# Constant matmuls in TensorE's early gaps, first scores in three bank pairs, output weights issued later

## The chip, the cores and the metric

The kernel runs on one core of one Trainium2 chip. The metric is the device time of one execution in microseconds (us). The kernel before takes 421.52 us, the median of eight runs between 418.97 and 425.11.

The engines of the core work in parallel, each through its own list of instructions in a fixed order: TensorE (PE in the profile; PEld is its weight load), VectorE (DVE), ScalarE (ACT), GpSimd (POOL) and SyncE (SP). The last two issue most of the DMA transfers here. TensorE writes its sums to PSUM, which has eight banks; DVE and ACT carry them from there to SBUF.

## The reference

Attention with a squared ReLU in place of the softmax, and then a gated feed-forward layer. There are 8 batches, 12 heads, 448 positions of width 64; the model width is 768 and the hidden width 1536.

```python
scores = scale * np.matmul(q, k.transpose(0, 1, 3, 2))      # scale = 1/sqrt(64)
attn = np.maximum(scores, 0.0) ** 2 / S                      # S = 448
attn_out = np.matmul(attn, v)
x = attn_out.transpose(0, 2, 1, 3).reshape(B * S, H * D)     # 3584 x 768
gate = np.maximum(x @ w_gate, 0.0)
val = x @ w_val
out = gate * val @ w_out                                     # 3584 x 768
```

## The kernel before, in words

**Units of work.** The four heads of a batch that are worked on together are a quad; there are three quads in each of the eight batches. One attention unit is a quad with its 448 query columns. Batch 0 is cut in two parts, the first 192 columns and the other 256, so that work can begin when only a part of q is in SBUF. For a unit the kernel does the following.

- k and q come from DRAM by GpSimd's DMA queue (`load_qk`, line 377, and `dma_in`, line 341), which also turns them to bf16. They are laid out with positions on the partitions and have to be transposed. In batches 0 and 1 TensorE does that (`transpose_first`, line 427, whose matmuls are at line 439; `transpose_pe`, line 455, matmuls at line 464), and DVE or ACT copy the result out of PSUM (lines 413 and 415). From batch 2 on, a DVE copy (the "perm" copy, line 485) and a DMA transpose on SyncE's queue (line 491) do it.
- Scores: seven tiles for a unit, each of four 64x64 matmuls that share the array (line 536). A tile takes a pair of PSUM banks. A ReLU carries it to SBUF (ACT line 546, or DVE line 548), and a square follows there (ACT line 557, or DVE line 559).
- P·V: 28 matmuls over the seven tiles (line 574), and a copy to x (ACT line 589, DVE line 591).

**Feed-forward.** `gv_plain` (matmuls at line 634) makes the gate and value products of batches 0 and 1 in 128-row blocks of the hidden width, with a ReLU on ACT (line 642) and a product on DVE (line 644). Later batches are taken in pairs with seven block products instead of eight (`gv_strassen`, line 734); the output product does the same (`out_both`, line 835). For this, sums and differences of the weights are made once by DVE: those of the gate and value weights into the buffer gvT at line 657 (before that, gvT holds early k, q and v), those of the output weights into the buffer woT at line 674, once all four pieces of the output weights are in SBUF.

**Loads.** All loads from DRAM stand in one list that GpSimd issues in order. It holds batch 0's k and q, its v, the late part of q, then the six pieces of gate and value weights (384 KB each) with batch 1 in between, batch 2's first quad, two pieces of output weights (576 KB each), batch 2's second quad, the other two pieces, batch 2's third quad, and the rest quad by quad. From batch 2 on, there is one buffer for raw k and q, so GpSimd waits for the perm copy before it issues the next quad's, and what stands behind it in the list waits too.

**Order.** The order of every engine is made when the program is built, by a planner (`Planner`, line 56, and `plan`, line 135). It keeps one clock for each engine, assigns a start to each operation from estimated lengths, and at each step commits the operation that can start first. DVE and ACT compete for ReLUs, squares and copies; `BIAS` is added to DVE's end when they are compared. TensorE's choice between attention and feed-forward goes by a share: the feed-forward work that remains before a goal, less `RESERVE` for that segment, is spread over the attention operations before the goal. On the chip only the order remains; the starts come from semaphores.

**PSUM.** Banks are given by the planner. `PAIRS`, `MORE_PAIRS` and `FIRST_PAIRS` are lists of first banks of a pair, for two, three and four pairs:

```python
PAIRS, MORE_PAIRS, FIRST_PAIRS = [0, 2], [0, 2, 4], [0, 2, 4, 6]
```

The whole early work (first transposes, both parts of batch 0's scores and P·V) takes pairs from all four before the change.

Of the kernel before, what the change touches and what calls it, by code (L numbers as in the profile page):

```python
# [55 lines left out]
class Planner:  # L56
    NOUT = 8
    SWITCH = 0.1
    BIAS = 0.3
    MARGIN = 4.0  # L60
    LATE = 3.0
    RESERVE = (1e3, 8.0, 4.0)
    WINDOW, ATT_WINDOW, START, AHEAD = 3, 2, 2.0, 2.0

    def __init__(self):
        self.t = {}
# [65 lines left out]
        self.ops.append(op)  # L132


def plan(first, att, ffn, others, pool, goals):

# [30 lines left out]
    while any(first) or att or ffn or active or pi < len(pool):  # L169
# [47 lines left out]
                cands.append((F[0], F[2], 2, "PE", ffn[F[3]][0]))  # L217
        assert cands, f"no operation can start: {ai} {len(ffn)} {len(active)} {pi}"
        s, _, kind, e, op = min(cands, key=lambda c: c[:3])
        P.commit(op, s, e)  # L220
        done(op)
        if kind == 0:
# [24 lines left out]
def kernel(  # L247
# [74 lines left out]
    def pe(emit, t, **kw):  # L322
        return Op({"PE": (t, t + 0.2)}, emit, **kw)
# [11 lines left out]
    def bank2(among=None):  # L335
        return Buf(r_ps, among if among is not None else PAIRS, width=2)
# [4 lines left out]
    def dma_in(dst, src, n_desc, us, deps=(), alloc=()):  # L341
        op = Op({"POOL": (0.5 + 0.0004 * n_desc,) * 2}, lambda: nc.gpsimd.dma_start(out=dst(), in_=src),  # L342
                deps=deps, alloc=alloc)
        op.load = us
        pool_ops.append(op)
        return op
# [30 lines left out]
    def load_qk(b, g):  # L377
        st = quads[(b, g)] = Quad()
        hs = slice(4 * g, 4 * g + 4)
        early = b < NEARLY  # L380
        st.raw_buf = None if early else Buf(r_raw)
        st.raw = lambda: early_raw(b, g) if early else raw_t[st.raw_buf.idx]
        src = lambda x, t0=0, t1=NT: x[b, hs].rearrange("h (p t) d -> p h t d", t=NT)[:, :, t0:t1]
        k_op = dma_in(lambda: st.raw()[64:128], src(k), 256, 1.15, alloc=[] if early else [st.raw_buf])
        if b == 0:
            st.load_q = lambda t0, t1: dma_in(lambda: st.raw()[0:64, :, t0:t1], src(q, t0, t1), 256, 0.17 * (t1 - t0))
            q_op = st.load_q(0, QT)
        else:
            q_op = dma_in(lambda: st.raw()[0:64], src(q), 256, 1.15)
        st.qk_ops = [k_op, q_op]  # L390
# [36 lines left out]
    def transpose_first(g):  # L427

        st = quads[(0, g)]
        st.qt_buf = Buf(r_qt)  # L430
        ps2, ps2b = bank2(FIRST_PAIRS), bank2(FIRST_PAIRS)

        def emit(ps2, part):
            raw = st.raw()
            for j in range(2):
                for t in range(NT) if part == 0 else range(QT, NT):
                    p0, p1 = (64 if t >= QT else 0, 128) if part == 0 else (0, 64)
                    for h2 in range(2):
                        nc.tensor.transpose(ps_b[64 * h2:64 * h2 + 64, ps2.idx + j, t * 128 + p0:t * 128 + p1],  # L439
                                            raw[p0:p1, 2 * j + h2, t, :], ident[p0:p1, p0:p1])  # L440

        op = pe(lambda: emit(ps2, 0), 0.9, deps=st.qk_ops + [id_op], alloc=[ps2, st.qt_buf])
        kcp = copy_qk(op, ps2, qk_cols(st, 0, NT, 1), qk_banks(ps2, 0, NT, 1), ((0.6, 0.72), (0.83, 0.98)))
        qcp = copy_qk(op, ps2, qk_cols(st, 0, QT, 0), qk_banks(ps2, 0, QT, 0), ((0.30, 0.42), (0.40, 0.55)))
        st.qt_ops = {0: [kcp, qcp]}

        def rest():
            op = pe(lambda: emit(ps2b, 1), 0.45, deps=[st.q_late], alloc=[ps2b])
            cp = copy_qk(op, ps2b, qk_cols(st, QT, NT, 0), qk_banks(ps2b, QT, NT, 0), ((0.37, 0.5), (0.51, 0.66)))
            st.qt_ops[HALF] = [kcp, cp]  # L450
            return op

        return op, rest
# [471 lines left out]
    def make_ident():  # L925
# [5 lines left out]
        for i in range(4):  # L931
            for c0, c1 in ((0, 32 * i), (32 * i + 32, 128)):
                if c0 < c1:
                    nc.vector.memset(ident[32 * i:32 * i + 32, c0:c1], 0.0)

    id_op = Op({"DVE": (1.5, 1.6)}, make_ident)
    others.append(id_op)
    for g in range(NQ):
        load_qk(0, g)
    for g in range(NQ):  # L940
# [8 lines left out]
            load_v(1, "abc".index(x))  # L949
    load_qk(2, 0)  # L950
    load_v(2, 0)
    for par in range(2):
        for hf in range(2):
            load_out(par, hf)
        load_qk(2, 1 + par)
        load_v(2, 1 + par)
    for b in range(3, B):
        for g in range(NQ):
            load_qk(b, g)
            load_v(b, g)  # L960


    att = []
    done_at = {}
    A_ = [Attention(0, g, 0, HALF, FIRST_PAIRS) for g in range(NQ)]
    A_ += [Attention(0, g, HALF, S - HALF, FIRST_PAIRS) for g in range(NQ)]
    A_ += [Attention(b, g, pairs=MORE_PAIRS if b < 4 else PAIRS) for b in range(1, B) for g in range(NQ)]

# [20 lines left out]
    for n in range(NQ, len(A_)):  # L989
        if n < 2 * NQ:  # L990
            att.append(late[n - NQ]())
        for i in range(NT):
            att.append(A_[n].s(i))
            if i == 1 and n not in (NQ, 2 * NQ):
                PV(n - 1)
            if i == 1 and n >= 2 * NQ - 1:
                T(n + 1 - NQ)
        if n in (2 * NQ - 1, len(A_) - 1):
            PV(n)
        if n == 2 * NQ - 1:  # L1000
            part_two = len(att)
# [10 lines left out]
        out_both(2 * p, p + 2, To_ops)  # L1012
        goals.append(done_at.get(2 * p + 3))

    for op in plan(first, att, ffn, others, pool_ops, goals):
        op.emit()


# [28 lines left out]
```

## Time and profile before

| | |
|---|---|
| median of eight runs | 421.52 us (418.97 to 425.11) |
| profiled execution | 419.79 us, of which the span from first to last instruction is 418.0 us |
| TensorE busy | 396.0 us, 95% of the span |
| DVE, ACT busy | 324.0 us (77%), 264.6 us (63%) |
| mean granted TensorE clock | 0.994 |
| DMA | 43.44 MB, 104 GB/s over the span |

The page of a profile cuts the span into 40 equal slices and shows for each, in tenths, how busy an engine was. The lists of instructions in order of time have the start, the length, the engine, the line, the operation with what it writes and reads, and in brackets the idle time before it with what ended that. Matmuls of one row may overlap, and the end of a matmul is modelled: the time from one start to the next tells more than one length.

### The profile page before, as it was taken

How to read it: one execution, taken by the hardware profiler on the slowest of the kernel's cores; microseconds unless marked ns; L12 is line 12 of the kernel's file. 1: busy time of each engine (PE TensorE's matmuls, PEld its weight loads, DVE VectorE, ACT ScalarE, POOL GpSimd, SP SyncE). 2: the span in 40 equal slices, each digit the busy share in tenths (PEclk: the TensorE clock that was granted, in tenths of full speed). 3: DMA queues.
4: the chain of work that ended last, by engine and by line, in shares of the span. 5: the costliest groups of instructions: out<-in, count | busy, mean ns of one | idle time of the engine just before them, and what ended most of it. 6: DMA issues, size and time to landing. Idle time of an engine off the chain costs nothing.

```text
span 418.0 us, 8710 instructions
## 1 busy us (share of the span) xinstructions
PE 396.0 (95%) x3444; PEld 208.9 (50%) x3444; DVE 324.0 (77%) x585; ACT 264.6 (63%) x408; POOL 73.9 (18%) x119
## 2 busy tenths in 40 slices
PE   3797999989999999999999999999999999999995
PEld 2475665434455544444445554444445555555562
DVE  1758777997699988999888779888878847677552
ACT  2778876987586876877864568776665443433221
POOL 7736303222111222211111022201000000000000
PEclk9999899999999999999999999999999999999999
DMA  8999989975579999789869778654002340000144
GB/s 117 184 199 200 200 136 166 154 101 78 83 100 180 154 184 126 79 92 103 112 88 107 162 143 147 87 68 64 1 2 59 94 115 0 2 0 2 39 114 114
DMA packets 75737, 43.44 MB, mean 104 GB/s; under 512 B 37808, under 2 KB 75696, under 8 KB 75696
## 3 DMA queue, kind: packets, MB, share of 16 engines
q0 software_dynamic: 33328, 23.60, 42.1%
q1 hardware_dynamic: 42368, 19.28, 27.6%
q8 instruction: 27, 0.44, 0.4%
q14 instruction: 14, 0.11, 0.1%
HBM read 47.19 MB, written 11.01 MB: 139 GB/s over the span
## 4 chain that ended last, share of the span: by engine, by line
PE 88%; DMA 4%; ACT 4%; DVE 2%; issue 1%; POOL 0%; DVEq 0%; ACTq 0%; POOLq 0%
PE ps L734 35%; PE ps L835 24%; PE ps L634 12%; PE ps L536 9%; PE ps L574 7%; DMA qkT<-perm 2%; ACT at L546 1%; DMA gvT<-in_q_dram 1%; ACT qkT L413 1%; PE ps L439 1%; PE ps L464 1%; DVE at L548 1%; DVE qkT L415 1%; ACT at L557 1%; POOL gvT L342 0%
## 5 line engine op out<-in xcount | busy, mean ns | idle before, releaser
L546 ACT ACTIVATE at<-ps 128x896 bf16<-128x896 f32 (+2 forms) x125 | 100.6, 845 | 21.5 <-PE ps L536 21.2
L683 ACT COPY f<-ps 128x448 f32<-128x448 f32 x101 | 53.3, 533 | 46.7 <-PE ps L734 43.9
L559 DVE TENSOR_TENSOR at<-at 128x896 bf16<-128x896 bf16 (+2 forms) x123 | 66.3, 562 | 6.4 <-ACT at L546 5.7
L548 DVE TENSOR_SCALAR at<-ps 128x896 bf16<-128x896 f32 (+2 forms) x64 | 61.7, 969 | 5.7 <-PE ps L536 5.5
L557 ACT ACTIVATE at<-at 128x896 bf16<-128x896 bf16 (+2 forms) x66 | 58.3, 892 | 5.0 <-DVE at L548 4.3
L536 PE MATMUL ps<-qkT 64*64 64x448 bf16 (+2 forms) x756 | 55.0, 353 | 5.5 <-ACT qkT L413 1.7
L734 PE MATMUL ps<-xT,gvT 128*128 128x448 bf16 x216 | 52.8, 353 | 0.5 <-ACT f L683 0.5
L734 PE MATMUL ps<-sx,wv 128*128 128x448 bf16 x216 | 52.8, 353 | 0.0
L734 PE MATMUL ps<-xT,wg 128*128 128x448 bf16 x216 | 52.5, 353 | 0.0
L734 PEld LDWEIGHTS <-gvT 128*128 128x128 bf16 x324 | 30.4, 98 | 31.8 <-issue 5.3
L835 PE MATMUL ps<-wo,hT 128*128 128x384 bf16 x240 | 44.1, 326 | 0.0
L835 PEld LDWEIGHTS <-hT 128*128 128x128 bf16 x312 | 29.9, 98 | 22.5 <-issue 3.1
L685 ACT ACTIVATE f<-ps 128x384 f32<-128x384 f32 x37 | 18.2, 493 | 36.1 <-PE ps L835 33.4
L342 POOL DMA_DIRECT2D vv<-in_v_dram x44 | 26.3, 608 | 74.8 <-PE ps L536 65.4
L835 PEld LDWEIGHTS <-sh 128*128 128x128 bf16 x288 | 27.2, 98 | 21.5 <-issue 3.8
L536 PEld LDWEIGHTS <-qkT 64*64 64x64 bf16 x756 | 19.6, 108 | 34.6 <-issue 27.9
L574 PE MATMUL ps<-at,vv 64*64 64x448 bf16 (+2 forms) x700 | 35.8, 345 | 0.3 <-ACT at L557 0.3
L634 PE MATMUL ps<-xT,wg 128*128 128x448 bf16 (+2 forms) x180 | 32.5, 316 | 2.2 <-ACT xT L589 1.5
L342 POOL DMA_DIRECT2D raw<-in_k_dram x18 | 11.3, 626 | 120.7 <-DVE perm L485 120.1
L634 PE MATMUL ps<-xT,wv 128*128 128x448 bf16 (+2 forms) x180 | 32.2, 315 | 0.0
L825 DVE SCALAR_TENSOR_TENSOR o<-ps,f 128x384 f32<-128x384 f32 x40 | 22.2, 554 | 11.8 <-PE ps L835 8.9
L734 PEld LDWEIGHTS <-wg 128*128 128x128 bf16 x216 | 20.4, 98 | 20.9 <-issue 3.2
(60 smaller groups left out, 479.9 us busy)
## 6 DMA issues: line engine op xcount, KB each, us to landing
out_dram<-o SPq DMA_DIRECT2D x112, 96.0 KB, 2.2
vv<-in_v_dram POOLq DMA_DIRECT2D x44, 112.0 KB, 5.8
raw<-in_k_dram POOLq DMA_DIRECT2D x18, 224.0 KB, 4.8
raw<-in_q_dram POOLq DMA_DIRECT2D x18, 224.0 KB, 6.7
wg<-in_moe_w_gate_dram POOLq DMA_DIRECT2D x6, 384.0 KB, 9.7
wv<-in_moe_w_val_dram POOLq DMA_DIRECT2D x6, 384.0 KB, 10.8
wo<-in_moe_w_out_dram POOLq DMA_DIRECT2D x4, 576.0 KB, 10.9
gvT<-in_k_dram POOLq DMA_DIRECT2D x6, 224.0 KB, 8.1
```

The costliest lines, as they stand in the source:

```text
L342: op = Op({"POOL": (0.5 + 0.0004 * n_desc,) * 2}, lambda: nc.gpsimd.dma_start(out=dst(), in_=src), deps=deps, alloc=alloc)
L536: nc.tensor.matmul(ps[64 * j:64 * j + 64, ps2.idx + h2, :n], lhsT=self.k_of(j, h2, i), rhs=self.q_of(j, h2), start=True, stop=True)
L546: nc.scalar.activation(self.at_of(i), src, AF.Relu)
L548: nc.vector.tensor_scalar_max(self.at_of(i), src, 0.0)
L557: nc.scalar.activation(at, at, AF.Square)
L559: nc.vector.tensor_tensor(at, at, at, ALU.mult)
L574: nc.tensor.matmul(ps[64 * h2:64 * h2 + 64, ps2.idx + j, :n], lhsT=st.v_of(j, h2, c), rhs=self.at_of(c)[64 * j:64 * j + 64, h2, :], start= ...
L634: nc.tensor.matmul(ps[:, pb.idx, :n], lhsT=w[:, kd, fc], rhs=xT_t[xbuf[b].idx][:, kd, cols], start=(kd == 0), stop=(kd == KD - 1))
L683: nc.scalar.copy(dst, src)
L734: nc.tensor.matmul(ps[:, pb.idx, :S], lhsT=w(g)[:, fc], rhs=rhs, start=start and g == 0, stop=stop and g == KH - 1, skip_group_check=True)
L825: op = Op({"DVE": V384}, lambda: nc.vector.scalar_tensor_tensor(o_t[ob.idx], ps[:, pb.idx, :OH], float(out_scale), f_t[fb.idx][:, :OH], AL ...
L835: nc.tensor.matmul(ps[:, pb.idx, :OH], lhsT=lhs(kf), rhs=rhs(kf), start=start and kf == 0, stop=kf == FH - 1, skip_group_check=True)
```

## The change

There are four parts.

1. **Fillers.** The planner gets a function `filler`. When the operation that it has chosen for TensorE could start only after a gap, and its planned start is below `FILL_UNTIL` (21 us on the planner's clock), it first commits a number of full-array matmuls (128x128 weights, up to 448 columns) that write to bank 6 or 7 and that nobody reads. Their operand is a stretch of ones in woT, set by one new DVE memset; woT's own contents are written much later. The columns are counted at 1200 a us while the planner's clock is below `FILL_COLD` (4 us), and at 2400 after. In the built program there are 48 such matmuls: 11 of 443 columns ahead of everything, 5 of 393 after the first quad's transposes, three groups of 3 (373, 439 and 428 columns) up to the second score tile of the second quad, then one or two between most score tiles (250 to 400), 7 of 418 ahead of the third P·V, and one of 243 ahead of the first gate matmul.
2. **Bank pairs.** The first transposes and the first part's scores and P·V take three pairs, so banks 6 and 7 stay free for the fillers. The second part keeps four.
3. **Loads.** The pieces of the output weights are spread: one, batch 2's second quad, two, batch 2's third quad, one.
4. **Planner's numbers.** `BIAS` 0.3 to 0.2; `RESERVE` 8 and 4 to 4 and 3; the estimated transfer of the second quad's k 1.15 to 2.4. `PV_AT` and `T_AT` name a 1 that stood in the code.

The planner makes a new order of all engines from this. In the early part it moves the second quad's transposes behind five of the first quad's seven score tiles, and the third quad's behind all seven; before, the second quad's came ahead of all score tiles and the third quad's after three.

```diff
-    BIAS = 0.3
+    BIAS = 0.2
-    RESERVE = (1e3, 8.0, 4.0)
+    RESERVE = (1e3, 4.0, 3.0)
+    FILL_FROM, FILL_COLD, FILL_UNTIL, FILL_MARGIN = 0.4, 4.0, 21.0, 0.1
...
         s, _, kind, e, op = min(cands, key=lambda c: c[:3])
+        if e == "PE" and s < P.FILL_UNTIL:
+            t0 = max(P.t.get("PE", 0.0), P.FILL_FROM)
+            gap = s - t0 - P.FILL_MARGIN
+            f = filler(gap, t0 < P.FILL_COLD) if gap > 0.1 else None
+            b = f.alloc[0].pick(t0) if f is not None else None
+            if b is not None and b[0] <= t0:
+                P.commit(f, t0, "PE")
+                P.mode = op.mode
         P.commit(op, s, e)
...
-        k_op = dma_in(lambda: st.raw()[64:128], src(k), 256, 1.15, alloc=[] if early else [st.raw_buf])
+        k_op = dma_in(lambda: st.raw()[64:128], src(k), 256, 2.4 if (b, g) == (0, 1) else 1.15,
+                      alloc=[] if early else [st.raw_buf])
...
-        ps2, ps2b = bank2(FIRST_PAIRS), bank2(FIRST_PAIRS)
+        ps2, ps2b = bank2(MORE_PAIRS), bank2(FIRST_PAIRS)
...
+    still = woT.rearrange("p a f m -> p (a f m)")
+    still_op = Op({"DVE": (0.2, 0.3)}, lambda: nc.vector.memset(still[:, :S], 1.0))
+    def filler(us, cold):
+        pb = bank([6, 7])
+        total = int(us * (1200 if cold else 2400))
+        n = (total + S - 1) // S
+        width = max(64, total // n)
+        def emit():
+            for _ in range(n):
+                nc.tensor.matmul(ps[:, pb.idx, :width], lhsT=still[:, :128], rhs=still[:, :width], start=True, stop=True)
+        return pe(emit, us, deps=[still_op], alloc=[pb], reads=[pb])
...
-    for par in range(2):
-        for hf in range(2):
-            load_out(par, hf)
-        load_qk(2, 1 + par)
-        load_v(2, 1 + par)
+    load_out(0, 0)
+    load_qk(2, 1)
+    load_v(2, 1)
+    load_out(0, 1)
+    load_out(1, 0)
+    load_qk(2, 2)
+    load_v(2, 2)
+    load_out(1, 1)
...
-    A_ = [Attention(0, g, 0, HALF, FIRST_PAIRS) for g in range(NQ)]
+    A_ = [Attention(0, g, 0, HALF, MORE_PAIRS) for g in range(NQ)]
```

## The prediction

> **What bounds the kernel now.** I read the page's slices first, then stretches, TensorE in order of time, GpSimd's queue, and the chain of work that ended last.
>
> ```profile
> PE   3797999989999999999999999999999999999995
> DVE  1758777997699988999888779888878847677552
> ACT  2778876987586876877864568776665443433221
> PEclk9999899999999999999999999999999999999999
> ```
>
> TensorE has room in the first five slices (52 us) and in the last one; in between it is the bound. The stretches give the size (the column after the lengths is TensorE's busy time):
>
> ```profile
> 0.00:10.45 10.45, 3.47 (x66) 2.58 (x68) 1.90 (x11) 2.22 (x3) 8.08 (x17) 1.00 0.87 117
> 10.45:20.90 10.45, 7.54 (x131) 4.46 (x127) 7.89 (x24) 8.14 (x19) 8.18 (x12) 1.00 1.35 184
> 20.90:31.35 10.45, 9.47 (x188) 8.00 (x183) 5.62 (x15) 7.84 (x18) 4.12 (x6) 1.00 1.39 199
> 31.35:41.80 10.45, 8.02 (x190) 6.21 (x184) 8.82 (x19) 9.16 (x19) 6.39 (x9) 0.97 1.39 200
> 41.80:52.25 10.45, 9.54 (x130) 7.21 (x128) 8.35 (x14) 8.71 (x14) 4.13 (x6) 0.87 1.35 200
> ```
>
> 38.0 of 52.25 us are busy, so 14.2 us stand idle there; from 60 us to the last output matmul the list of TensorE's waits holds only 3.0 us. What a change saves before 50 us arrives at the end nearly whole; later there is little to save. The fourth-last and last columns matter too: the clock column says 1.00 until 41 us, and DMA moves 180 to 200 GB/s from 10 us on. TensorE in order of time contradicts the clock column:
>
> ```profile
> 5.66 1.70 PE L439 MATMUL ps<-ident,gvT 128*64 128x128 bf16 x28 [5.66 <-DMA gvT<-in_q_dram]
> ...
> 19.97 2.45 PE L574 MATMUL ps<-at,vv 64*64 64x192 bf16 x56
> ...
> 24.33 0.72 PE L634 MATMUL ps<-xT,wg 128*128 128x192 bf16 x6
> 24.90 0.66 PE L634 MATMUL ps<-xT,wv 128*128 128x192 bf16 x6
> ...
> 37.80 0.97 PE L464 MATMUL ps<-ident,gvT 128*64 128x128 bf16 x28
> ...
> 41.75 1.71 PE L464 MATMUL ps<-ident,gvT 128*64 128x128 bf16 x28
> ```
>
> 28 transposes take 0.97 us at 37.80 and 1.71 us at 41.75, where the granted clock reads 0.50 to 0.54. The first transposes take 1.70, although the column says 1.00 there: they run at half speed. So does the first P·V: 14 rounds of four 192-column matmuls in 2.3 us are 0.163 us a round, 192 columns at 1.2 a ns; at 24.90 six 192-column matmuls start 0.082 us apart, 2.4 a ns. Half speed therefore lasts from 5.66 to about 24 us, and again from 41.0 to 44.5.
>
> GpSimd's queue tells when weights land, since in the built program each issue waits for the transfer eight before it:
>
> ```profile
> 19.37 0.60 POOL L342 DMA_DIRECT2D gvT<-in_v_dram  x1 [1.34 <-DMA wg<-in_moe_w_gate_dram]
> 21.37 0.59 POOL L342 DMA_DIRECT2D gvT<-in_v_dram  x1 [1.40 <-DMA wv<-in_moe_w_val_dram]
> ...
> 38.16 0.59 POOL L342 DMA_DIRECT2D vv<-in_v_dram  x1 [0.76 <-PE ps L536]
> 39.30 0.59 POOL L342 DMA_DIRECT2D vv<-in_v_dram  x1 [0.55 <-PE ps L536]
> ...
> 64.26 1.72 POOL L342 DMA_DIRECT2D wo<-in_moe_w_out_dram  x2
> ```
>
> The first gate and value pieces land at 19.37 and 21.37, one 384 KB piece every 2.0 us. By the same order of eight, k and q of batch 1's second quad land by 38.16 and 39.30 (the scores named there were long done). These times are DMA's own; the change leaves their order.
>
> ```profile
> 75.21 10.39 DMA qkT<-perm
> 85.60 0.04 issue
> 85.64 0.57 PE ps L536 x8
> ```
>
> In the chain, one DMA transpose of 10.39 us is the only large wait after 60 us; TensorE stands 1.28 us for it.
>
> **The change, step by step.**
>
> *Fillers.* 48 matmuls of 128x128 constants. First 11 of 443 columns, from about 1.1 us (DVE starts at 0.83; its new memset of 448 columns is near the 0.17 us row of the 128x128 one). At half speed 11 x 443 / 1.2 = 4.06 us, ending at 5.2, before the data at 5.63: free. The other 37 have 12,898 columns: 5.4 us at full speed, 10.7 us at half. They stand ahead of scores, P·V and transposes in TensorE's fixed order, so what overruns its gap delays these.
>
> Is the clock full by then? The Trainium skill (TensorE: Matmul & The Clock Gate, Part 1) has a free-running 3.4 us activity window and says not to care: the ramp costs under 1% of a typical span. By that rule one window at half speed is the whole loss, at most 1.7 us. The rows say otherwise: scores in small bursts kept it half for 18 us. The lost time is 3 x 0.65 us in transposes and about 1.8 us in P·V (21 rounds of 0.163 instead of 0.080). I go by the rows. The window does bear on the filler: 4.06 us covers a whole window only for some phases, so I take full speed from about 7 us, and half speed until 14 as the bad end. Part 4 of the same page says that transposes do not engage the full clock; 0.97 against 1.71 us contradicts it here.
>
> *First scores in three bank pairs and the new order.* Before, the second quad's transposes came ahead of all scores, and the third quad's (12.23) waited for a bank pair. Now five of the first quad's seven score tiles come ahead of the second quad's transposes, two more ahead of the third's. Walk: transposes at 5.66, about 1.5 us; the two copies still follow each other, now DVE 896 (0.62, row at 54.91) then ACT 384 (0.48) instead of 0.91 + 0.36; scores at 8.4 instead of 9.98, first relu at 8.6 instead of 11.22. Five tiles pass while the second quad's data (landed 8.65) waits; its transposes run at about 9.6, copies to 11.6; the third's need the pair these copies free: 11.7 to 12.6. The eighth tile starts at 12.6; before it was at 16.1. From there ACT has about ten relus at 0.39 (4.32/11), three squares at 0.52 and a copy: 6.0 us, to 18.7; DVE's 4 relus of 0.53, 15 squares of 0.28 and copy come to the same. The last two tiles' P·V (0.6) and x copy (0.5) end near 20.9, instead of 24.7. With three pairs rather than four, two relus still run side by side, which is all that the engines can do; I cost it at nothing, and at up to 1 us if a late relu stops the order. At half speed until 14 us the fillers take 1.64, 0.93 and 1.10 us in these gaps and the eighth tile comes at 15.4: 0.6 us gained in all.
>
> *What is late next.* The first value matmul (24.90) can move to 21.4 where its weights land: 3.5 us. The next weights (25.37 against a use at 29.07, 29.37 against 33.76) allow as much. Batch 1's second quad, used at 41.75 and landed at 39.30, allows 2.45: TensorE then stands about 1 us there. So 2.45 us is carried on. The half-speed spell at 41 to 44.5 lies past the fillers' end. It costs 0.7 (transposes) + 0.3 (scores) + 0.35 (P·V) = 1.4 us, and whether it returns depends on how idle gaps fall in the window: 0 to 1.4, I take 0.7, as two ends equally near.
>
> *Output weights.* The four 576 KB pieces were issued two at 48 and two at 64 us; now it is one, two, and the last behind batch 2's third quad at about 75. It adds 576 KB at 197 GB/s, 2.9 us, to the DMA time beside the 10.39 us transpose. If both share, the wait of 1.28 us grows by up to 2.9; if the transpose is ahead, by nothing, and a lighter queue at 48 can shorten it to a gain of 0.5. I take 0.6 lost, nearer to the small end: only its tail overlaps.
>
> *BIAS, RESERVE, the k estimate.* They add no instruction but re-deal work: 67 relus from PSUM on DVE instead of 64; 2.6 and 4.6 us more FFN matmuls ahead of two P·Vs of batch 1. There TensorE idled only 0.2 us (50 to 60), so nothing to win; 3.0 us of waits after 60 could vanish or double. From -1.5 to +3; I take 0.
>
> *Sum.* 419.79 (span 418.0 and 1.8 around it) - 2.45 - 0.7 + 0.6 = **417.2**. The eight runs fall into 418.97 to 420.26 (with the profiled one) and 422.78 to 425.11; the median, 421.52, lies between the groups and no view shows what parts them. I forecast 417.2 for the median too, as the cold start is the part that could differ run by run; if the groups recur it is 418.9.
>
> **Rivals.** (1) *More*: the spell at 41 us vanishes whole and the landing at 39.30 is no hindrance because copies and relus catch up meanwhile: 3.5 + 1.4 gives 414.9. For it: the idle 0.92 us at 45.5 waits for an ACT copy. Against: TensorE's order is fixed there. (2) *Swallowed*: weights and data land as before, the clock stays half until 14, or stage two stays bound by ACT and DVE (8.82 and 9.16 of 10.45 us): 0 to 0.6 us gained, 419.2 to 421.5. (3) *Slower*: DVE reaches the differences of the output weights (line 674) before the last piece has landed and, being in order and full (75 to 95 us: 19.8 of 20), holds back every hidden-tile product. The piece is issued near 75 and lands in 9.4 to 12.6 us, by 87.6; DVE gets there about 4.8 us after the third perm copy (86.63 less 2.6), at 88.8. From a landing 13.8 us after issue it costs; beyond 16.4 it eats the gain; 22.3 us would make it 425.7. Against it: no such transfer took over 12.6.
>
> **Numbers.** Forecast 0.60 (own range 415 to 419.5, about half of it under 417.3), more 0.22, swallowed 0.12, slower 0.06. About 1% (4.2 us) is what these runs can tell from no change. Faster 0.28 + 0.22 = 0.50, same 0.44, slower 0.06. Range 413.8 to 421.5: down to rival 1 with 1 us of re-dealing, up to rival 2's end.
>
> **What would show it.** Right: transposes near 1 us from the second quad on; first relu near 8.6; eighth tile near 12.6; first value matmul near 21.4, waiting for DMA; transposes of batch 1's second quad near 39.4, waiting for DMA; TensorE full from 47 us about 3 us sooner. Wrong: fillers or the P·V at 0.16 us a round after 14 us; a wait over 3 us at the second DMA transpose of batch 2; DVE idle ahead of line 674.

## The result, and the profile after

The changed kernel takes 417.97 us, the median of 22 executions, where the kernel before takes 422.21 (59 executions in the same comparison). The ratio is 0.992, with a 95% interval from 0.9894 to 0.9946. So the change saves 0.8%, some 3.3 us of the kernel before: the interval excludes no change, but the gain is under the 1% that the prediction took as the least that these runs can tell. Ratios and intervals here use only the executions within 1.5% of the fastest of their kernel, the medians all of them, so that a ratio is not the quotient of two medians. One execution of each kernel lay far off (584.96 us at a mean granted clock of 0.655, and 517.8).

The others scatter by 6 to 7 us, with TensorE's mean granted clock. In a second comparison, 21 of 55 executions of the kernel before have a clock of 0.996 or more and a median of 419.3 us, and the others 423.5; of 20 of the changed kernel, nine have such a clock and 417.1 us, and the others 419.1. Among the executions at 0.996 or more the change is thus worth 2.2 us.

The profile below is of an execution of the changed kernel that took 419.0 us, with a span of 417.2. In the spans the gain over the profiled execution before (418.0) is only 0.8 us; one execution in the middle of the scatter says little by its length, but its rows say where time went. First the page's slices, TensorE, DVE, ACT and clock:

```profile
PE   8997999989999998999999999999999999999995
DVE  4759686989799988989788879898986847677552
ACT  3678677876677777876675668776756644433221
PEclk9999999999999999999999999999999999999999
```

TensorE now looks busy from the first slice on, but part of that is constants. In stretches (length; TensorE's busy time first, then weight loads, DVE, ACT, GpSimd, granted clock, DMA share, GB/s):

```profile
0.00:10.45 10.45, 8.62 (x95) 4.27 (x99) 4.30 (x18) 3.50 (x6) 7.87 (x17) 1.00 0.88 115
10.45:20.90 10.45, 9.52 (x180) 5.18 (x179) 7.55 (x20) 7.21 (x18) 8.34 (x12) 1.00 1.36 187
20.90:31.35 10.45, 9.41 (x191) 7.62 (x189) 6.30 (x15) 7.90 (x19) 3.52 (x5) 1.00 1.39 199
31.35:41.80 10.45, 8.12 (x172) 6.57 (x175) 9.46 (x20) 9.06 (x17) 6.02 (x9) 0.92 1.39 199
41.80:52.25 10.45, 10.39 (x118) 7.41 (x120) 6.60 (x12) 6.47 (x12) 4.26 (x7) 0.92 1.35 200
```

46.06 us are busy of 52.25, where it was 38.03; but 12.2 of the 46.06 are the constants. TensorE in order of time (start, length, instruction, idle time ahead):

```profile
1.39 4.25 PE L962 MATMUL ps<-woT 128*128 128x443 bf16 x11 [1.39 <-DVE woT L949]
5.79 1.18 PE L451 MATMUL ps<-ident,gvT 128*64 128x128 bf16 x28
...
9.52 1.07 PE L451 MATMUL ps<-ident,gvT 128*64 128x128 bf16 x24
...
11.88 1.03 PE L451 MATMUL ps<-ident,gvT 128*64 128x128 bf16 x22 [0.40 <-DVE qkT L427]
...
17.36 0.28 PE L548 MATMUL ps<-qkT 64*64 64x192 bf16 x4
17.57 0.39 PE L962 MATMUL ps<-woT 128*128 128x250 bf16 x2
...
19.05 1.32 PE L586 MATMUL ps<-at,vv 64*64 64x192 bf16 x56
...
20.39 1.41 PE L962 MATMUL ps<-woT 128*128 128x418 bf16 x7
21.73 0.77 PE L586 MATMUL ps<-at,vv 64*64 64x192 bf16 x28
...
23.29 0.66 PE L646 MATMUL ps<-xT,wv 128*128 128x192 bf16 x6
...
40.09 1.70 PE L476 MATMUL ps<-ident,gvT 128*64 128x128 bf16 x28 [0.88 <-DVE at L571]
41.73 1.71 PE L586 MATMUL ps<-at,vv 64*64 64x256 bf16 x28
...
43.64 0.89 PE L646 MATMUL ps<-xT,wg 128*128 128x256 bf16 x6
```

The first 28 transposes take 1.18 us (1.70 before), 22 of the third quad's 1.03 (1.53 before): from the second quad on the clock is full. P·V runs 14 rounds in 1.32 us (2.45 before). The first value matmul is at 23.29, 1.6 us sooner, and TensorE goes over to the feed-forward blocks of 256 columns at 43.64, where it did at 46.41, with 24 score tiles done behind the first value matmul where it had done 26. Two tiles are some 0.5 us (12 matmuls, three tiles, take 0.7), so it is 2.3 us ahead. At 40.09 the transposes take 1.70 us again; the second half-speed spell has not gone. Later, waits come back:

```profile
73.25 0.57 PE L548 MATMUL ps<-qkT 64*64 64x448 bf16 x8 [1.27 <-DMA qkT<-perm]
...
86.52 0.57 PE L548 MATMUL ps<-qkT 64*64 64x448 bf16 x8 [0.74 <-DMA qkT<-perm]
```

Before, TensorE waited for a DMA transpose once in the whole span; now three times, 3.2 us in all. Between 56 and 100 us it stands 2.33 us, where it stood 1.29. DVE, in the same kernel, makes the copies that feed these transposes:

```profile
60.41 0.62 DVE L497 COPY perm<-raw 128x1792 bf16<-128x1792 bf16 x1
...
73.33 0.63 DVE L497 COPY perm<-raw 128x1792 bf16<-128x1792 bf16 x1 [1.48 <-DMA qkT<-perm]
...
86.60 0.63 DVE L497 COPY perm<-raw 128x1792 bf16<-128x1792 bf16 x1 [1.40 <-DMA qkT<-perm]
```

The second and third copies wait until the transposes of the copy before them have read the buffer. The third starts at 86.60; before the change at 86.63. TensorE had been 2.3 us ahead at 44 us; this chain had gained nothing by its third copy.

### The profile page after: what moved, and what is told of

Same layout as the page of the kernel before. It is cut to its first block, busy times and chain, and to the rows that moved or that the text cites. A ratio compares the mean times of both kernels' runs of the same rounds, so it can differ in the third digit from the quotient of the medians.

```text
span 583.2 us, 8812 instructions
## 1 busy us (share of the span) xinstructions
PE 573.6 (98%) x3492; PEld 249.9 (43%) x3492; DVE 338.0 (58%) x586; ACT 269.6 (46%) x408; POOL 73.9 (13%) x119
## 4 chain that ended last, share of the span: by engine, by line
PE 97%; DVE 1%; ACT 1%; DMA 1%; issue 0%; POOL 0%; POOLq 0%
PE ps L746 37%; PE ps L847 25%; PE ps L646 14%; PE ps L548 9%; PE ps L586 9%; PE ps L962 1%; PE ps L451 1%; DMA gvT<-in_q_dram 1%; PE ps L476 0%; DVE at L560 0%; ACT qkT L425 0%; ACT at L558 0%; DVE qkT L427 0%; POOL gvT L353 0%; DVE xT L603 0%
## 5 line engine op out<-in xcount | busy, mean ns | idle before, releaser
L746 PE MATMUL ps<-sx,wv 128*128 128x448 bf16 x216 | 74.4, 468 | 0.0
L746 PE MATMUL ps<-xT,gvT 128*128 128x448 bf16 x216 | 74.4, 469 | 0.0
L746 PE MATMUL ps<-xT,wg 128*128 128x448 bf16 x216 | 74.2, 469 | 0.0
L548 PE MATMUL ps<-qkT 64*64 64x448 bf16 (+2 forms) x756 | 64.1, 407 | 1.4 <-DVE qkT L427 1.1
L847 PE MATMUL ps<-wo,hT 128*128 128x384 bf16 x240 | 63.6, 429 | 0.0
L586 PE MATMUL ps<-at,vv 64*64 64x448 bf16 (+2 forms) x700 | 48.1, 433 | 0.2 <-DVE at L560 0.2
L646 PE MATMUL ps<-xT,wv 128*128 128x448 bf16 (+2 forms) x180 | 46.4, 412 | 0.0
L646 PE MATMUL ps<-xT,wg 128*128 128x448 bf16 (+2 forms) x180 | 44.4, 402 | 0.9 <-ACT at L558 0.6
L746 PEld LDWEIGHTS <-wv 128*128 128x128 bf16 x216 | 24.5, 118 | 36.5 <-issue 34.5
L803 DVE CUSTOM_DVE_ANT_0 g<-ps,f 128x448 bf16<-128x448 f32 x36 | 22.5, 624 | 30.2 <-PE ps L746 27.6
```

The source lines that it names most:

```text
L548: nc.tensor.matmul(ps[64 * j:64 * j + 64, ps2.idx + h2, :n], lhsT=self.k_of(j, h2, i), rhs=self.q_of(j, h2), start=True, stop=True)
L586: nc.tensor.matmul(ps[64 * h2:64 * h2 + 64, ps2.idx + j, :n], lhsT=st.v_of(j, h2, c), rhs=self.at_of(c)[64 * j:64 * j + 64, h2, :], start= ...
L646: nc.tensor.matmul(ps[:, pb.idx, :n], lhsT=w[:, kd, fc], rhs=xT_t[xbuf[b].idx][:, kd, cols], start=(kd == 0), stop=(kd == KD - 1))
L746: nc.tensor.matmul(ps[:, pb.idx, :S], lhsT=w(g)[:, fc], rhs=rhs, start=start and g == 0, stop=stop and g == KH - 1, skip_group_check=True)
L803: cur["g1"] = Op({"DVE": V448}, lambda pb=cur["D"], f=u2, gb=cur["g1b"]: nc.vector._custom_dve(dve_ops.TENSOR_ADD_SAT, out=g_t[gb.idx], in ...
L847: nc.tensor.matmul(ps[:, pb.idx, :OH], lhsT=lhs(kf), rhs=rhs(kf), start=start and kf == 0, stop=kf == FH - 1, skip_group_check=True)
```

## The experiments

Each ratio is against executions of the kernel before on the same chip, taken together with those of the variants. Three chips were used, and the kernel before took 421.87 us on the first (the changed kernel again, no_fill, start_alone, wo_early), 423.06 on the second (drop_small, late_fill, no_retune, perm2) and 423.6 on the third (retune_alone, bias_only, wo_early_2, late_wo). The table has the rows that the text uses, from each kernel's profile: start of the first value matmul, start of the transposes of batch 1's second quad with the length of 28 of them, DVE's third permuting copy, TensorE's waits for DMA transposes.

| kernel | first value | batch 1, second quad | third copy | waits | span | median (n) | ratio, 95% |
|---|---|---|---|---|---|---|---|
| before | 24.90 | 41.75 (1.71) | 86.63 | 1.3 | 418.0 | | 1 |
| changed, again | 23.29 | 40.09 (1.70) | 86.60 | 3.2 | 417.2 | 417.9 (20) | 0.9951, 0.992 to 0.9981 |
| no_fill | 25.77 | 42.54 (0.97) | 91.31 | 5.0 | 420.5 | 423.23 (20) | 1.0026, 0.9992 to 1.006 |
| start_alone | 24.93 | 41.48 (0.97) | 87.58 | 5.2 | 421.7 | 422.96 (20) | 1.0023, 0.9991 to 1.0054 |
| wo_early | 23.97 | 40.11 (0.97) | 86.57 | 2.4 | 415.8 | 416.33 (4) | 0.9882, 0.9803 to 0.996 |
| wo_early_2 | 22.95 | 39.49 (1.70) | 86.10 | 1.4 | 415.6 | 417.7 (12) | 0.9922, 0.988 to 0.9965 |
| drop_small | 23.56 | 39.70 (0.97) | 87.94 | 5.5 | 419.5 | 420.69 (10) | 0.9987, 0.9941 to 1.0033 |
| late_fill | 23.18 | 40.20 (0.97) | 86.08 | 2.9 | 415.3 | 418.81 (10) | 0.992, 0.989 to 0.9949 |
| no_retune | 25.67 | 42.22 (0.97) | 85.83 | 2.5 | 418.9 | 423.13 (10) | 1.0032, 0.9992 to 1.0072 |
| retune_alone | 22.70 | 39.05 (0.97) | 84.31 | 1.0 | 414.1 | 417.56 (12) | 0.9921, 0.988 to 0.9961 |
| bias_only | 23.13 | 39.27 (0.97) | 88.20 | 4.6 | 418.4 | 420.84 (12) | 0.999, 0.9947 to 1.0034 |
| late_wo | 23.17 | 40.20 (0.97) | 84.41 | 1.5 | 414.9 | 416.49 (10) | 0.9896, 0.9854 to 0.9938 |

**The changed kernel again.** Not edited; it gives the profile shown above.

> The changed kernel as it is, for a profile at the full clock. Theory of the prediction: transposes near 1 us from the second quad on, first relu near 8.6 us, eighth score tile near 12.6, first value matmul near 21.4 waiting for its weights, transposes of batch 1's second quad near 39.4 waiting for DMA, TensorE full from 47 us; 417 to 418 us. Rival (the gain is lost on the way, or comes from elsewhere): first value matmul as early, but the transposes of batch 1's second quad within 1 us of 41.75.

It took 417.9 us. Its ratio is 0.9951, and its interval (0.992 to 0.9981) overlaps that of the first comparison (0.9894 to 0.9946).

**No constants.** The order is that of the changed kernel, but the fillers emit nothing.

```diff
-            for _ in range(n):
+            for _ in range(0):
```

> The changed kernel with the fillers' matmuls left out and every other instruction in the same order. Theory clock (the fillers' full clock is what saves): the first P.V at 0.16 us a round again, transposes 1.6 us, and most of the gain gone, within 1 us of the kernel before. Theory order (the new order of scores and transposes saves, the clock little): half speed until about 24 us, but first relu near 8.6 and the eighth tile near 14, and a gain of 2 us or more kept.

```profile
9.90 1.54 PE L451 MATMUL ps<-ident,gvT 128*64 128x128 bf16 x22
...
19.72 2.45 PE L586 MATMUL ps<-at,vv 64*64 64x192 bf16 x56
...
25.77 1.17 PE L646 MATMUL ps<-xT,wv 128*128 128x192 bf16 x6
```

TensorE in order of time: at half speed from the first transposes to the first value matmuls (six of 192 columns take 1.17 us, then 0.66), and the whole gain is gone. In this order of work the constants are needed, and their effect is the clock.

**The first filler alone.** The kernel before with only the 11 matmuls of 443 columns ahead of the transposes.

```diff
+    def warm_emit():
+        for _ in range(11):
+            nc.tensor.matmul(ps[:, 7, :443], lhsT=still[:, :128], rhs=still[:, :443], start=True, stop=True)
+    warm = Op({"PE": (0.1, 0.2)}, warm_emit, deps=[still_op])
...
+    trans = [warm, *trans]
```

> The kernel before with only the first eleven 443-column constant matmuls put ahead of its transposes. Theory clock: the first transposes or those of the second quad run in 1 us, but the clock falls back in the gaps that follow; P.V at 0.16 again; 0 to 1 us gained. Rival (one busy window is enough[...]): full speed from about 7 us to the end, P.V at 0.08 us a round, 2 us gained. If neither: no speed gained and no time.

```profile
1.39 4.25 PE L943 MATMUL ps<-woT 128*128 128x443 bf16 x11 [1.39 <-DVE woT L937]
5.57 1.69 PE L439 MATMUL ps<-ident,gvT 128*64 128x128 bf16 x28
...
19.88 2.45 PE L574 MATMUL ps<-at,vv 64*64 64x192 bf16 x56
```

In this execution 4.25 us of constants, right up to the transposes, leave them at half speed (1.69 us), and P·V as well. In the changed kernel the same filler was followed by 1.18. No time is gained: 422.96 us. The profiled execution, at a mean clock of 0.998, is not like most: of the 19 others 18 have 0.970 to 0.983, where the kernel before has 0.984 to 1.0. So the filler did change the granted clock, but how fast the first transposes and P·V ran in those 18 no profile shows. A burst at the start without the fillers behind it is worth nothing here.

**Small gaps unfilled.** Fillers of gaps under 0.3 us emit nothing.

```diff
-            for _ in range(n):
+            for _ in range(n if us > 0.3 else 0):
```

> The changed kernel without the fillers of gaps under 0.3 us (the 250- to 400-column ones between score tiles and the last one of 243), everything else in order. In the changed kernel's profile eleven score tiles from 14.2 us on come 0.53 us apart with TensorE busy throughout; without fillers it was 0.36. Theory (TensorE's fillers and its changes between 64x64 and full-array matmuls pace these tiles): 0.35 to 0.40 us a tile, first P.V near 17.2 to 17.8 instead of 19.05, first value matmul near 21.7. The end moves by less than 0.5 us, since the second quad of batch 1 still waits for its data near 40. Rival (they hold the clock): the clock falls to half before P.V, P.V at 0.16 us a round, first value matmul no earlier than 23.3, the end 1 us later or more.

```profile
14.42 1.60 PE L548 MATMUL ps<-qkT 64*64 64x192 bf16 x20 [0.41 <-ACT qkT L425]
16.21 2.14 PE L548 MATMUL ps<-qkT 64*64 64x192 bf16 x24 [0.19 <-DVE at L560]
18.29 2.40 PE L586 MATMUL ps<-at,vv 64*64 64x192 bf16 x56
...
42.45 0.97 PE L646 MATMUL ps<-xT,wg 128*128 128x256 bf16 x6
```

I had expected the tiles to come closer, and they did: 0.35 us apart, eleven in 3.87 us, where the fillers made it 4.82 (0.53 from one to the next where a filler stands between). But the clock fell in that stretch, P·V took 2.40 us, and the value matmul came at 23.56, no sooner than with the fillers (23.29). So far the rival was right: the small fillers cost about 0.2 us where one stands between two tiles, 1 us in all, and hold the clock for it. That this is why the kernel ends later (420.69 us) is not shown. In its profile TensorE goes over to the blocks of 256 columns at 42.45, 1.2 us ahead of the changed kernel, whose profile has the half-speed spell at 40 us; behind that it stands 5.5 us for DMA transposes, where the changed kernel stands 3.2. And its interval (0.9941 to 1.0033) overlaps that of the changed kernel again.

**The second half-speed spell.** Three constant matmuls of 448 columns ahead of batch 1's first score tile, three ahead of the transposes of its second quad.

```diff
+            if (b, g) == (1, 1):
+                fill_bank(ps2.idx, 3)
...
+                if (self.b, self.g, i) == (1, 0, 0):
+                    fill_bank(ps2.idx, 3)
```

> The changed kernel with six more constant matmuls of 448 columns: three ahead of batch 1's first score tile, three ahead of the transposes of its second quad, where TensorE stood 0.9 us. Theory (the half-speed spell near 41 us comes from these gaps, and parts the runs of the changed kernel into 416 to 418.5 and 420.5 to 422): no spell, fewer runs over 420, median 0.5 to 1.5 us lower. Rival (the spell is not in the gaps, or comes back a window later): the same spread; the six matmuls cost up to 0.5 us.

28 transposes take 0.97 us at 40.20 and there is no spell. The median is 418.81 us, the ratio 0.992, as for the changed kernel, with a narrower range: 417.09 to 420.25, against 416.16 to 422.01. But the profiles of seven kernels that have nothing against it show the transposes at full speed as well, and wo_early lacks the spell where wo_early_2, the same kernel, has it. It comes and goes from one execution to the next. The six matmuls cost 1.5 us of TensorE, about what the spell was estimated at.

**The loads back in their old order.**

```diff
-    load_out(0, 0)
-    load_qk(2, 1)
...
-    load_out(1, 1)
+    for par in range(2):
+        for hf in range(2):
+            load_out(par, hf)
+        load_qk(2, 1 + par)
+        load_v(2, 1 + par)
```

> The changed kernel with the output weights' four pieces loaded where the kernel before loads them. Theory of the prediction (the late piece costs 0.6 us at the second DMA transpose of batch 2): 0.5 us faster than the changed kernel, the wait for that transpose about 1.3 us shorter or gone. Rival (spreading the pieces takes pressure off the perm copies and helps): 0.5 to 2 us slower than the changed kernel, with a longer wait for batch 2's k and q.

The first timing, 416.33 us, had four executions; the repeat had twelve.

> The changed kernel with the order of loads of before, again, as its first timing rested on four executions. If the later output weights cost the 0.6 us that the prediction took: about 417.3, 0.6 under the changed kernel. If they cost nothing: 417.5 to 418.5. If they are worth something: over 418.5. The waits for the DMA transposes of batches 2 and 3 (1.4 and 0.6 us) stay as in its first profile.

417.7 us in the repeat, against 417.9 and 417.97 for the changed kernel in other comparisons: no difference that these runs can show. The wait for the transposes does not go with the late piece either: with the old order it is 2.4 and 1.4 us, with the new 3.2.

**Two permuting buffers.** N_PERM 2 instead of 1, and four output buffers instead of five to make room.

```diff
-    N_QT, N_AT, N_X, N_F, N_G, N_O = 3, 10, 3, 5, 4, 5
-    N_RAW, N_PERM, N_VV = 1, 1, 3
+    N_QT, N_AT, N_X, N_F, N_G, N_O = 3, 10, 3, 5, 4, 4
+    N_RAW, N_PERM, N_VV = 1, 2, 3
```

> The changed kernel with two buffers for the perm copy instead of one (and four output buffers instead of five, for the room). TensorE's order stays as it is up to the fourteenth P.V. In the changed kernel's profile the waits for DMA transposes are 3.2 us against 1.3 before, and the perm copy waits for the transpose ahead of it. Theory (one perm buffer ties each transpose to the end of the last, and this chain takes back part of the gain): these waits under 1 us, 1.5 to 2.5 us faster than the changed kernel. Rival (the transposes are slow because the loads share the DMA engines, so that two at once only slow each other): waits of 3 us as before, no gain.

422.51 us in ten executions, five from 416.43 to 422.13 and five from 422.89 to 426.67. The ratio, 0.9895 (0.984 to 0.995), rests on the first five alone; the profile, with one wait of 5.1 us for a transpose, is of the slowest. The scatter is wider than the gain looked for, and the one change of buffers came with another: inconclusive.

**The planner's numbers back.** The changed kernel with BIAS 0.3 and RESERVE 8 and 4.

```diff
-    BIAS = 0.2
+    BIAS = 0.3
...
-    RESERVE = (1e3, 4.0, 3.0)
+    RESERVE = (1e3, 8.0, 4.0)
```

> The changed kernel with BIAS at 0.3 and RESERVE at 8 and 4 again. Theory of the prediction (they re-deal work and are worth nothing): within 1 us of the changed kernel. Rival (they give part of the gain, by the feed-forward moved ahead in batch 1 or the ReLUs dealt to DVE): 1 to 3 us slower than the changed kernel.

This was not expected: 423.13 us, nothing left of the gain, though fillers, bank pairs and loads are all there and the clock is full (P·V 1.35 us). The first value matmul is at 25.67, later than before the change. (bias_only below has the same kernel but for BIAS.)

**The planner's numbers alone.** The kernel before, with those two lines of the change and nothing else.

```diff
-    BIAS = 0.3
+    BIAS = 0.2
...
-    RESERVE = (1e3, 8.0, 4.0)
+    RESERVE = (1e3, 4.0, 3.0)
```

> The kernel before with BIAS 0.2 and RESERVE 4 and 3 only: no fillers, no third bank pair, the old order of loads. Theory one (these constants re-deal relus between DVE and ACT, which pays only where the early part is no longer held at half speed): first value matmul still near 24.9 us, time within 1% of before, 419 to 423. Theory two (the constants are the gain by themselves, as the loss on taking them back could say): 416 to 419, and TensorE's idle time after 50 us smaller. The prediction's own value was 0 with bounds from 1.5 us faster to 3 us slower.

The whole gain: 417.56 us, a ratio of 0.9921 (0.988 to 0.9961), with not one constant matmul. Its TensorE in order of time, after two rows of the kernel before that have not been shown yet:

```profile
12.23 1.53 PE L439 MATMUL ps<-ident,gvT 128*64 128x128 bf16 x22 [1.38 <-DVE at L548]
...
15.78 4.18 PE L536 MATMUL ps<-qkT 64*64 64x192 bf16 x56 [1.38 <-DVE at L548]
```

```profile
7.97 1.53 PE L439 MATMUL ps<-ident,gvT 128*64 128x128 bf16 x22 [0.76 <-DMA gvT<-in_q_dram]
...
10.89 1.53 PE L439 MATMUL ps<-ident,gvT 128*64 128x128 bf16 x22 [0.75 <-ACT qkT L413]
...
13.82 4.44 PE L536 MATMUL ps<-qkT 64*64 64x192 bf16 x56 [0.75 <-ACT qkT L413]
18.35 2.27 PE L574 MATMUL ps<-at,vv 64*64 64x192 bf16 x56
...
22.70 0.66 PE L634 MATMUL ps<-xT,wv 128*128 128x192 bf16 x6
...
39.05 0.97 PE L464 MATMUL ps<-ident,gvT 128*64 128x128 bf16 x28 [0.21 <-DVE at L548]
...
42.10 0.83 PE L634 MATMUL ps<-xT,wg 128*128 128x256 bf16 x6
```

The clock is half up to the first P·V (1.53 for the transposes, 2.27 for 14 rounds of P·V), and still the first value matmul comes at 22.70, ahead of the changed kernel. The copies tell why; first those of the kernel before, then DVE's and ACT's here:

```profile
10.42 0.91 ACT L413 COPY qkT<-ps 128x896 bf16<-128x896 bf16 x1 [2.11 <-PE ps L439]
...
11.36 0.36 DVE L415 COPY qkT<-ps 128x384 bf16<-128x384 bf16 x1 [2.66 <-ACT qkT L413]
11.63 1.01 DVE L548 TENSOR_SCALAR at<-ps 128x384 bf16<-128x384 f32 x2
```

```profile
9.71 0.62 DVE L415 COPY qkT<-ps 128x896 bf16<-128x896 bf16 x1 [1.83 <-PE ps L439]
10.25 0.55 DVE L548 TENSOR_SCALAR at<-ps 128x384 bf16<-128x384 f32 x1
```

```profile
10.36 0.48 ACT L413 COPY qkT<-ps 128x384 bf16<-128x384 bf16 x1 [1.98 <-DVE qkT L415]
10.74 0.88 ACT L546 ACTIVATE at<-ps 128x384 bf16<-128x384 f32 x2
```

With 0.1 us less against DVE, the planner gives it the copy of 896 columns (0.62 us; ACT took 0.91) and ACT the one of 384 (0.48), and relus follow on both. TensorE's two waits of 1.38 us for relus on DVE, at 12.23 and 15.78, become 0.75 each, for copies: 1.3 us. Another 0.7 is that k and q of the second quad land sooner in this execution (transposes at 7.97, not 8.68), which a setting of the planner does not explain. Together they are the 2.0 us between 15.78 and 13.82. The feed-forward blocks that began at 46.41 begin at 42.10, with the same 26 score tiles done: 4.3 us ahead, 2.2 from the first value matmul, the rest from later copies and from a second spell that this execution lacks. Of the 4.3, 3.9 arrive at the end of the span. Not all of the 4.3 is the edit's: 0.7 is the earlier landing, without which the first value matmul would stand near 23.4, level with the changed kernel, and up to 1.4 (the prediction's size of it) is the spell. This execution, 415.86 us, is also the second fastest of its twelve; the gain rests on their median, and the profile shows where it can come from. Theory two was right in time and theory one wrong about the 24.9; theory two's sign (less idle time of TensorE later) did not show: from 56 to 200 us it stands 3.0 us, against 2.5.

**RESERVE back, BIAS kept.**

```diff
-    RESERVE = (1e3, 4.0, 3.0)
+    RESERVE = (1e3, 8.0, 4.0)
```

> The changed kernel with RESERVE put back to 8 and 4, BIAS left at 0.2. The order of the first part is the same as in the changed kernel up to about 30 us. Theory one (what taking both back cost was the early deal of relus and copies, which BIAS sets): first value matmul at 23.3, time 416 to 419, as the changed kernel. Theory two (it was RESERVE, by the FFN matmuls kept ahead of P·V in batch 1): the early rows as in the changed kernel, but 420 to 423.

```profile
39.27 0.97 PE L476 MATMUL ps<-ident,gvT 128*64 128x128 bf16 x28 [0.22 <-DVE at L560]
...
72.67 0.57 PE L548 MATMUL ps<-qkT 64*64 64x448 bf16 x8 [1.67 <-DMA qkT<-perm]
...
88.12 0.57 PE L548 MATMUL ps<-qkT 64*64 64x448 bf16 x8 [2.93 <-DMA qkT<-perm]
```

The early rows are those of the changed kernel or better (39.27, and no spell), and 420.84 us come out. The time is lost in two waits for DMA transposes, 4.6 us. RESERVE sets how much feed-forward work is kept for later, so it may decide whether TensorE has something to do when the transposes are late. But that is argued from one profile, and the interval (0.9947 to 1.0034) still overlaps those of the changed kernel again and of wo_early_2.

This kernel and no_retune differ in BIAS alone (0.2 here, 0.3 there), and show its part. The first copy of 896 columns is DVE's here (0.62 us, from 6.87) and ACT's there (0.91 us, from 6.74). The first value matmul, here and there:

```profile
23.13 0.66 PE L646 MATMUL ps<-xT,wv 128*128 128x192 bf16 x6
```

```profile
25.67 0.66 PE L646 MATMUL ps<-xT,wv 128*128 128x192 bf16 x6
```

It comes 2.5 us sooner with 0.2, and the blocks of 256 columns begin at 42.01 against 46.44. So with fillers the early lead goes with BIAS, and in retune_alone, without them, it goes with the same deal of the copies. At the end less is left: 420.84 us (0.999) against 423.13 (1.0032), with overlapping intervals. BIAS at 0.3 with the new RESERVE wasn't run.

**Both loose ends together.** The old order of loads and the matmuls against the second spell.

> The changed kernel with the order of loads of before and with three 448-column constant matmuls ahead of batch 1's first score tile and three ahead of the transposes of batch 1's second quad. If the clock's second drop at 40 us and the output weights are separate costs: 415.5 to 417.5, with few executions over 420 and the 28 transposes at 40 us in about 0.97 us. If the time is held by the chain of raw copy and DMA transpose after 60 us whatever comes before: 417.5 to 419, as the changed kernel.

416.49 us in ten executions from 414.89 to 419.47, a ratio of 0.9896. Only the median of four executions is lower. It is faster than the kernel before; its interval overlaps those of the changed kernel and of retune_alone, so that it beats these isn't shown. In its profile the third copy is at 84.41, as in retune_alone at 84.31.

## Why the prediction was right, and where it wasn't

The time was right: 417.97 for a forecast of 417.2, within the range. The reasons were right for the first 13 us and for the clock, and wrong about which part of the change pays.

In part the agreement is luck. The sum of the prediction starts from a profiled execution of 419.79 us and takes 2.55 off; it was carried over to the median because the cold start was thought to be what parts the executions, with 418.9 for the case that the two groups recur. They do recur: of 22 executions with a recorded clock, the far-off one aside, the 15 at 0.996 or more have a median of 417.3 us, and the other seven one of 421.2. And retune_alone, which keeps the cold start, has only three of twelve below 0.996. The 2.2 us among executions of like clock are the fairer measure of the 2.55. Why the share of low clocks differs from kernel to kernel stays open.

- *The clock.* Right, and shown by leaving the constants out: TensorE at half speed to 26 us without them, nearly full from the first transposes with them. The weighing of the row against the Trainium skill (TensorE: Matmul & The Clock Gate, Part 1 and Part 4) came out for the row: small bursts kept the clock half for 15 to 21 us in the three kernels without fillers (the kernel before, no_fill and retune_alone), far beyond one activity window of the page, and 28 transposes run in 0.97 or 1.7 us. The latter contradicts Part 4 only as far as the speed of transposes goes; whether they count as work that brings the full clock, which the page denies too, no run here shows.
- *The walk to the eighth tile.* Right to 0.2 us: first relu 8.53 (8.6), second quad's transposes 9.52 (9.6), third's 11.88 (11.7), eighth tile 12.72 (12.6). The first filler ended at 5.64, not 5.2, in part as its memset took 0.43 us and not 0.17; a cost of that is not shown, since behind the same filler the transposes began at 5.47 to 6.53 us. The walk had the new deal of the first copies in it (0.62 on DVE, then 0.48 on ACT, for 0.91 and 0.36), but booked it under the bank pairs and the new order. It goes with BIAS, as bias_only and no_retune show.
- *First value matmul at 21.4.* Wrong: 23.29. The sum took ACT and DVE as the limit behind 12.6, and for the fillers said only that what overruns its gap delays. They do overrun: with a filler between two tiles these come 0.53 us apart (17.36 and 17.89), against 0.30 for the 14 tiles before. Over the eleven tiles that is about 1 us (4.82 against 3.87 in drop_small). And 1.41 us of constants stand at 20.39, ahead of the last P·V; as DVE ends the last square that this P·V needs only at 21.69, they delay it by an estimated 0.6 us at most, its own length. So the mis-sized term is most likely the price of the 37 fillers, which was taken at 0 and comes to 1 to 1.7 of the 1.9 us. No run parts it from the other terms, since without the small fillers the clock falls.
- *Batch 1's second quad at 39.4, 2.45 carried.* Nearly right: 40.09 here, 39.27, 39.49 and 40.11 in kernels that differ only later. TensorE was 2.3 us ahead at 44 us, near the 2.45. The next sentence, that what is saved before 50 us arrives nearly whole, failed in this profile: 2.3 us became 0.8, of which 1.0 went into waits between 56 and 100 us. In retune_alone it held (3.9 of 4.3). Whether it holds hangs on TensorE's waits behind 60 us.
- *The spell at 41 us.* 0 to 1.4, taken at 0.7: it is there in two of the three profiles of the changed kernel with either order of loads, not in the third. As a mean the value stands.
- *Output weights, 0.6 lost.* Not shown: with the old order 417.7. The added wait for transposes came (3.2 us in all, where I had 1.9), but also with the old loads. The marks of a loss by this edit did not come: the longest wait for a transpose is 1.3 us, and DVE reaches the differences of the output weights at 91.35 without standing ahead of them (rival 3).
- *BIAS and RESERVE at 0, from -1.5 to +3.* This is the step that failed. Taken back, they cost the whole gain; alone, they bring the whole gain. The prediction looked for their effect only behind 50 us, in the re-dealt relus and the reserved feed-forward work, and overlooked that BIAS also deals the first copies and relus, which TensorE waited for at 12.23 and 15.78, 2.8 us together. As the walk had counted the new deal elsewhere, the sum came out well, and its largest term, the early start, was credited to the wrong part of the change.

So the parts do not add up: constants with the new bank pairs and order, without the two numbers, 1.0032; the numbers with that order but without constants, 1.0026; the numbers alone, 0.9921; everything, 0.992. On top of the two numbers, fillers, bank pairs and loads together gain nothing that these runs can show. The reading that fits is that the new order with three pairs costs about as much at half clock as the constants give back; it is argued, since neither the bank pairs nor the estimate for k were run alone.

The profiles account for the spans by two terms that can be read off TensorE's rows: when it goes over to the blocks of 256 columns (brought to 26 score tiles done by 0.25 us a tile), and its idle time behind 60 us, as the rows list it.

| kernel | blocks of 256 columns from | idle behind 60 us | span less both |
|---|---|---|---|
| before | 46.4 | 3.0 | 368.6 |
| changed, again | 44.1 | 4.1 | 369.0 |
| no_fill | 45.3 | 5.9 | 369.3 |
| start_alone | 45.7 | 7.1 | 368.9 |
| wo_early | 43.4 | 3.8 | 368.6 |
| wo_early_2 | 43.5 | 3.3 | 368.8 |
| drop_small | 43.0 | 6.2 | 370.4 |
| late_fill | 42.7 | 3.8 | 368.9 |
| no_retune | 45.9 | 3.2 | 369.8 |
| retune_alone | 42.1 | 3.4 | 368.6 |
| bias_only | 42.5 | 5.7 | 370.2 |
| late_wo | 42.7 | 3.6 | 368.7 |

In nine of the twelve the rest is the same within 0.8 us. So no_fill ends 6.4 us behind retune_alone because it is 3.2 us later at these blocks and stands 2.5 us more behind 60. The early lead is set by the order and the clock; how much of it is kept, by the idle time.

What stays open: what sets that idle time, and with it the phase of the chain of raw copy, permuting copy and transpose. The third copy is at 84.3 and 84.4 in the two shortest spans and at 91.3 in one of the longest, but it doesn't order the ones between (85.83 with 418.9, 86.57 with 415.8). The run that was to cut the chain, with two buffers, settled nothing. Also open is the rest of 370 us in drop_small, bias_only and no_retune.

## What to carry to other kernels

Run a change's tuning constants alone before crediting its main idea: here two numbers of the planner, which were costed at nothing, gave by themselves what the whole change gave. Constant matmuls do raise the clock, but each change of array mode between bursts costs time, so they pay where the engine is idle anyway. A gain ahead of a chain of buffer copies and DMA transposes can be lost in waits for it: count the engine's idle time behind it too.

## What the runs showed of the hardware

The clock can be lost in stretches with work every 0.35 us: in drop_small the score tiles from 14.42 to 18.29 us came at that spacing, and P·V behind them ran at half speed, though the transposes at 12 us (22 in 1.03 us) had been at full. The same 4.25 us of full-array matmuls was followed by transposes at nearly full speed in one execution (28 in 1.18 us, the changed kernel) and nearly at half in another (1.58 us, drop_small), though the instructions up to there are the same. So 1.69 us in start_alone's one profile says little of that kernel.

A 128x128 matmul between two tiles of 64x64 ones costs more than its columns: two of 250 columns are 0.21 us at full speed and a tile's four of 192 are 0.08, but the pair takes 0.53, so some 0.24 us goes into the changes between them (an estimate from these starts). Where no change follows, nothing is added: behind the filler of 243 columns at 22.68 the gate matmuls, also 128x128, start 0.11 us later, which is its columns. The Trainium skill (TensorEngine Tiling (Array Packing), Key Properties) says that a change of tiling mode drains TensorE, and gives no price; this is one, for two changes.

And the granted clock as the profile's column has it was 1.00 from 0 to 20 us in every profile of the table but drop_small's, whether their first transposes ran at half speed or full; there only the lengths of the instructions told. A fall from the full clock does show in it: 0.85 in drop_small from 10 to 20 us, and 0.81 in the kernel before from 38 to 47.
